# Transposed weights in a two-layer decode backward pass: turned by TensorE, or by the DMA on the way in

## The chip, the cores and the metric

The kernel runs on one core of a Trainium2 chip. The time is that of one execution on the device, in microseconds (us), and a kernel's time is the median of its runs. Engines are written as in the profile: PE is TensorE's matmul queue and PEld its weight loads, DVE is VectorE, ACT is ScalarE, POOL is GpSimd, SP is SyncE. SP issues all loads here and POOL issues all stores; both use the core's 16 DMA engines.

## The reference

Two layers of attention and MLP with the same weights and the same K/V caches, one query token for each of two batch rows, and then the gradient of everything. All tensors are bf16.

```python
x = A_x                                     # [2, 1, 1024]
x = x + A(ln(x), k_cache, v_cache, wq, wo)  # layer 0: attention
x = x + B(ln(x), w1, b1, w2, b2)            # layer 0: MLP
x = x + A(ln(x), k_cache, v_cache, wq, wo)  # layer 1
x = x + B(ln(x), w1, b1, w2, b2)            # layer 1
# A: q = x @ wq -> 32 heads of 128; k_cache, v_cache [2, 4, 16384, 128], 8 query heads per kv head
#    softmax(q k^T / sqrt(128)) v, then @ wo [4096, 1024]
# B: gelu(ln(x) @ w1 [1024, 3584] + b1) @ w2 [3584, 1024] + b2
# outputs: x, and the gradients of A_x, k_cache, v_cache, wq, wo, w1, b1, w2, b2 for a given grad_out
```

The products are thin (two columns), so the work is moving weights and caches through the chip: each K and V cache is read once in every pass of each layer, and the gradients of both caches, 33.5 MB each, are written at the end.

## The kernel before, in words

**Chunks and slots.** All that is read from HBM comes in chunks of up to 1 MB, 128 partitions by 4096 bf16. The program is first recorded as a list of pieces by `emit(fn, uses)`, each naming the chunks that it uses. `Program.run` then walks the list: it gives chunks, in the order of their first use, to slots as these come free, and issues a chunk's load the moment that it has a slot. So the order of the loads on SP is the order of first use, and a load is issued as early as slots allow. There are 14 slot tiles, three more areas in `last`, and four borrowed from `e1` and `ds1` while these are not in use. In the last pass six of the slot tiles are taken over as staging for the stores. The order on every engine is the order of the list; no scheduler changes it. A load waits on SP for the readers of its slot, and for the load eight places earlier.

**Turning on TensorE.** A product with a transposed weight needs the weight with its rows and columns exchanged. TensorE makes that: eight 128x128 transposes against an identity into a PSUM bank (`tp`), and one copy of 128x1024 to SBUF, on ACT or DVE, whichever has less counted work (`copy_bf`, L192 and L195). K and V blocks are turned in the same way. There are two forms:

- `ablock` (with `turn_of`, L324): the turn is emitted at once into a small tile `kT`, and the product that uses it is put in a list, `pend`, and emitted two blocks later (`SKEW = 2`), so that the copy lies behind other work.
- `turned` and `turned_ahead` (L365): the turned block is copied back over the chunk in its own slot (L368 on ACT, or L192 and L195), and the product reads it from the slot later.

**The two passes back.** Layer 1's backward attention is `attn_bwd(1, ...)`, and layer 0's `attn_bwd(0, ...)`. Each has 128 steps, 16 for each of eight (batch, kv head) groups, and 13 more for the second half of the work, which lags by 13 steps (`LAG_B`). A step turns a block of V and multiplies it (L940), multiplies a block of K (L921), and in some steps takes a block of wo (L807) or of wq (L836): 8 blocks of each weight for each of the four kv heads. The wo blocks of the first kv head come before the steps, the wq blocks of the last kv head behind them (`tail_wq`).

In layer 1 the steps from 86 on also turn w2 in its slots (L365, with the forward product L1229). Between the layers come, in this order: the LayerNorm's backward sums (L395), the products with the turned w2 (`w2_use`, L1257), between them the turns of w1 (`w1_turned`), the products with the turned w1 (`w1_bwd`, L727), the MLP's LayerNorm with the turns of the first wo chunks and of V's first blocks in its gaps (`chain`), and the wo products (L807).

In layer 0 the steps also make the outputs: weight gradients (L1072) and cache gradients (L1025), each a matmul of 128x512 into PSUM, a cast to a staging tile on ACT or DVE (`cast_out`, L200 and L203), and a store of 512 KB from POOL (L1032, L1088).

The loads are these two helpers' (L291 and L296):

```python
nc.sync.dma_start(ap.rearrange("p (t d) -> p t d", d=128), src[g, :, c * 32:(c + 1) * 32, :])
nc.sync.dma_start(ap[:, 0:rb * n].rearrange("p (j n) -> p j n", j=rb),
                  W[j0 * 128:(j0 + rb) * 128, c0:c0 + n].rearrange("(j p) n -> p j n", p=128))
```

Of the kernel before, what the change touches and what calls it, by code (L numbers as in the profile page):

```python
# [21 lines left out]
SKEW = 2  # L22
# [81 lines left out]
def kernel(  # L104
# [70 lines left out]
    obanks = [half[1, 0], half[1, 1], sb[1][:]]  # L175
    st = {"tp": 0, "ob": 0, "blk": 0, "stg": 0, "qm": [0, 0], "act": 0.0, "dve": 0.0}

# [112 lines left out]
    def ld_kv(src, g, c):  # L290
        return P.chunk(lambda ap: nc.sync.dma_start(  # L291
            ap.rearrange("p (t d) -> p t d", d=128), src[g, :, c * 32:(c + 1) * 32, :]))

    def ld_rows(W, j0, rb, c0, n):

        return P.chunk(lambda ap: nc.sync.dma_start(  # L296
            ap[:, 0:rb * n].rearrange("p (j n) -> p j n", j=rb),
            W[j0 * 128:(j0 + rb) * 128, c0:c0 + n].rearrange("(j p) n -> p j n", p=128)))
# [41 lines left out]
    def ablock(tiles, use, uses, mids=(), hold=None):  # L340


        if hold is None:
            hold = {}
            emit(turn_of(tiles, hold), uses)
        for fn, us in mids:
            emit(fn, us)
        pend.append(lambda: use(hold["kT"]))
        while len(pend) > SKEW:
            emit(pend.pop(0))  # L350

    def aflush():
        while pend:
            emit(pend.pop(0))

# [18 lines left out]
    def as_tiles(dst, part):  # L374
        return dst.ap[:, part * 1024:(part + 1) * 1024].rearrange("p (a b) -> p a b", b=128)

    def turned_ahead(blocks, act=True):

        now, then = [], []
        for n, (tiles, use, uses) in enumerate(blocks):  # L380
            now.append(turned(tiles, uses, uses[0], n % 4, act))
            then.append((lambda use=use, c=uses[0], n=n: use(as_tiles(c, n % 4)), uses))
        return now, then

    def turned_wo(wo):
        now, then = turned_ahead(wo[0])
        return now, then + [(wo[1], ())]

# [138 lines left out]
    def attn_fwd(l, order, x_in, chunk_k, chunk_v, first=None, tail={}):  # L527
# [103 lines left out]
        for s in range(n_steps + 2):  # L631
# [36 lines left out]
            else:  # L668
                if pend:
                    emit(pend.pop(0))  # L670
                for fn, us in mids:
# [122 lines left out]
    def wo_bwd_blocks(l, k):  # L794

        ws = ld_wo(k)
        hold = {}

        def blk(r):
            c = ws[r // 4]  # L800

            def use(kT):
                if r == 0:
                    hold["raw"] = small.tile([128, 8, 2], F32, name="do_raw", bufs=2)
                ps = ob()[:, 0:2]
                for o in range(DJ):
                    PE.matmul(ps, lhsT=kT[:, o, :], rhs=gA_all[:, o, 2 * l:2 * l + 2], start=(o == 0),  # L807
                              stop=(o == DJ - 1))
                V.tensor_copy(out=hold["raw"][:, r, :], in_=ps)
                dve(0.15)  # L810

            return (lambda: [col(c, r % 4, 1024, o) for o in range(DJ)]), use, [c]

# [13 lines left out]
    def wq_bwd_blocks(l, k, first, acc):  # L827
        ws = ld_wq(k)

        def blk(j):  # L830
            c = ws[j // 4]

            def use(kT):
                ps = ob()[:, 0:2]
# [8 lines left out]

            return (lambda: [col(c, j % 4, 1024, r) for r in range(R)]), use, [c]

        return [blk(j) for j in range(DJ)]

    def attn_bwd(l, order, gT, chunk_v, first, outputs=None, after=None, extra={}, fill=()):
# [37 lines left out]
        for i, k in enumerate(kvs):  # L886
# [6 lines left out]
            if i + 1 < HKV:  # L893
                for n, b in enumerate(bl):
                    wb[32 * i + 18 + LAG_B + 16 + 2 * n] = b
            else:
                now, tail_wq = turned_ahead(bl, act=False)
                for n, p in enumerate(now):
                    extra[129 + n] = list(extra.get(129 + n, ())) + [p]

# [3 lines left out]
        while s <= n_steps or (outputs is not None and outputs(s, True)):  # L904
# [39 lines left out]
            else:  # L944
                for fn, us in side[:n] + mids + side[n:2 * n]:
                    emit(fn, us)
                if pend:
                    emit(pend.pop(0))
            rest = side[2 * n:]
            if s in wb:  # L950
                ablock(*wb.pop(s), mids=rest)
            else:
                for fn, us in rest:
                    emit(fn, us)
# [241 lines left out]

    emit(turn_round)
    wo_now, wo_then = turned_wo(wo_bwd_blocks(1, up[0] % HKV))
    for p in wo_now[:4]:
        emit(*p)  # L1200
    dmps = w1_bwd(1, w1T)
# [9 lines left out]
    v_now, v_first = turns_ahead(chunk_v(up[0], 0))  # L1211
    chain(g3_, 1, wo_now[4:] + v_now)
    for p in wo_then:
        emit(*p)
# [22 lines left out]
    for j, s_ in enumerate(turn_steps):  # L1237
        i = j // 4
        extra.setdefault(s_, [])
        if j % 4 == 0:  # L1240
            extra[s_].append(w2_last(i))
        extra[s_].append(turned(lambda j=j, i=i: [col(ws2c[i], j % 4, 1024, o) for o in range(DJ)], [ws2c[i]],
                                ws2c[i], j % 4, act=False))
    ws1c = ld_w1()
    attn_bwd(1, up, saved["g3"], chunk_v, v_first, extra=extra, fill=w1_turned(ws1c, 0, ws1c[0]))
    col_to_row(xM1, out_0.rearrange("b s d -> (b s) d"))

# [13 lines left out]
    for i in range(FJ // 4):  # L1261
        emit(*w2_use(i))
        for p in w1_turned(ws1c, i, ws1c[i], act=False) if 1 <= i < 6 else ():
            emit(*p)
    emit(lambda: V.tensor_tensor(out=dh_all[:, :, 0:2], in0=slopes[0][:], in1=dhps0, op=ALU.mult))
    for j in (6, 7):
        for p in w1_turned(ws1c, j, ws1c[j], act=False):
            emit(*p)
    dmps0 = w1_bwd(0, ws1c)
# [5 lines left out]

    wo_now, wo_then = turned_wo(wo_bwd_blocks(0, down[0] % HKV))
    v_now0, v_first0 = turns_ahead(chunk_v(down[0], 0))
    chain(g1_, 1, wo_now + v_now0)
    for p in wo_then:
        emit(*p)  # L1280
# [79 lines left out]
```

## Time and profile before

| what | value |
|---|---|
| median of 3 runs | 1194.04 us (1185.31 to 1196.43) |
| profiled execution, its own time | 1194.48 us |
| its span | 1192.7 us |
| PE busy | 1032.3 us (87%) |
| weight loads (PEld) | 859.1 us (72%) |
| DVE, ACT, POOL busy | 605.4, 554.8, 125.1 us |
| read from HBM, written | 352.37 MB, 98.62 MB, 378 GB/s over the span |
| transposes L324 from slots | 4224, 369.2 us of PE |
| loads of wq, wo, 1 MB each, to landing | 10.7 and 15.2 us (median, into slots) |

The forward passes take the first 460 us. Layer 1's backward attention lies at 480 to 680, the change of layers at 680 to 737, layer 0's backward attention with all the outputs at 737 to 1170, and the last stores behind it. A matmul's time in the rows is from issue to its modelled end, and neighbours overlap, so the distance between starts tells more than the mean. The busy share of the DMA engines counts the time in which packets are under way, and stands a little above 1 when all are in use; the rate beside it says what was moved.

### The profile page before, as it was taken

Reading aid. Unit: us, or ns where it says so; the run is one execution under the profiler, and the core shown is the slowest. Engines: PE = TensorE matmul, PEld = TensorE weight load, DVE = VectorE, ACT = ScalarE, POOL = GpSimd, SP = SyncE. Lnnn points to the kernel's source line nnn. Section 1 sums busy time; section 2 is a strip of 40 time slices with the busy share of each in tenths; the row PEclk is TensorE's granted clock in tenths of the full one; section 3 lists DMA queues with packets and bytes.
Section 4 is the critical chain, followed back from the end, with each engine's and each line's share of the span. In section 5 each row is a group of like instructions: output and inputs, shape, how many; then the busy total and the mean of one; then the engine's idle time right before and its main releaser. Section 6 shows DMA issues by size and latency. Waiting matters only on the chain. (4 is left out here: it accounts for less than half of the span.)

```text
span 1192.7 us, 44045 instructions
## 1 busy us (share of the span) xinstructions
PE 1032.3 (87%) x19762; PEld 859.1 (72%) x19805; DVE 605.4 (51%) x1266; ACT 554.8 (47%) x996; POOL 125.1 (10%) x214
## 2 busy tenths in 40 slices
PE   6878887689988988888889988988997998899996
PEld 6778786688988987888888886655565555555663
DVE  2423242224333333333434435877886787677775
ACT  2423241124333423333444424766775776567774
POOL 1000000000000000000000010322222222222222
PEclk9966695679787758889999997999998999899998
DMA  9999999989999996999999976899999999999994
GB/s 365 420 421 421 422 420 421 386 298 378 420 420 420 422 409 264 378 414 418 417 402 330 365 295 232 323 376 373 417 417 373 384 417 410 371 362 409 416 415 200
DMA packets 106041, 453.83 MB, mean 381 GB/s; under 512 B 8658, under 2 KB 8658, under 8 KB 75516
## 3 DMA queue, kind: packets, MB, share of 16 engines
q1 hardware_dynamic: 78780, 352.36, 74.5%
q0 software_dynamic: 27072, 98.66, 20.5%
q8 instruction: 154, 2.52, 0.8%
q14 instruction: 35, 0.29, 0.1%
HBM read 352.37 MB, written 98.62 MB: 378 GB/s over the span
## 5 line engine op out<-in xcount | busy, mean ns | idle before, releaser
L192 ACT COPY kT<-tp 128x512 int32<-128x512 int32 x427 | 250.0, 586 | 418.3 <-PE tp L324 391.0
L324 PE MATMUL tp<-ident,slot 128*128 128x128 bf16 x4224 | 369.2, 238 | 12.1 <-issue 5.1
L324 PEld LDWEIGHTS <-slot 128*128 128x128 bf16 x4224 | 284.4, 107 | 30.0 <-issue 12.3
L195 DVE COPY kT<-tp 128x1024 bf16<-128x1024 bf16 x209 | 144.5, 691 | 296.6 <-PE tp L324 240.8
L200 ACT CAST slot<-sc 128x512 bf16<-128x512 f32 x271 | 157.6, 589 | 50.2 <-PE sc L1072 19.6
L203 DVE CAST slot<-sc 128x512 bf16<-128x512 f32 x227 | 154.4, 688 | 38.1 <-PE sc L1025 18.6
L1025 PE MATMUL sc<-last 128*128 128x512 bf16 x324 | 119.7, 389 | 17.1 <-ACT slot L200 5.3
L921 PEld LDWEIGHTS <-slot 128*128 128x128 bf16 x1888 | 80.0, 98 | 42.5 <-issue 18.6
L940 PEld LDWEIGHTS <-kT 128*128 128x128 bf16 x2048 | 80.7, 97 | 38.5 <-issue 21.4
L1032 POOL DMA_DIRECT2D out_dram<-slot x128 | 69.0, 539 | 281.2 <-ACT slot L200 173.9
L203 DVE CAST slot<-sb 128x512 bf16<-128x512 f32 x126 | 86.7, 688 | 18.1 <-PE sb L1025 6.4
L664 PE MATMUL sc<-qd,kT 128*128 128x8 bf16 x2048 | 90.3, 171 | 2.6 <-issue 2.6
L940 PE MATMUL sc<-qd,kT 128*128 128x8 bf16 x2048 | 90.0, 170 | 1.7 <-issue 1.6
L200 ACT CAST slot<-sb 128x512 bf16<-128x512 f32 x128 | 75.3, 589 | 29.1 <-PE sb L1072 16.0
L664 PEld LDWEIGHTS <-kT 128*128 128x128 bf16 x2048 | 73.1, 99 | 3.0 <-issue 2.9
L1025 PE MATMUL sb<-last 128*128 128x512 bf16 x161 | 62.1, 386 | 6.6 <-ACT slot L200 1.6
L365 PE MATMUL tp<-ident,slot 128*128 128x128 bf16 x692 | 58.0, 239 | 6.2 <-issue 2.2
L647 PE MATMUL sb<-e,slot 128*128 128x8 bf16 x1280 | 56.7, 176 | 6.3 <-ACT e L583 3.8
L1072 PE MATMUL sc<-last 128*128 128x512 bf16 x155 | 56.6, 384 | 4.8 <-DVE last L1060 3.3
L647 PEld LDWEIGHTS <-slot 128*128 128x128 bf16 x1280 | 50.1, 102 | 9.6 <-issue 7.1
L365 PEld LDWEIGHTS <-slot 128*128 128x128 bf16 x692 | 48.2, 107 | 11.5 <-issue 9.0
L192 ACT COPY slot<-tp 128x512 int32<-128x512 int32 (+1 forms) x52 | 29.7, 574 | 52.9 <-PE tp L365 49.8
(292 smaller groups left out, 1258.7 us busy)
## 6 DMA issues: line engine op xcount, KB each, us to landing
slot<-in_A_k_cache_dram SPq DMA_DIRECT2D x101, 1024.0 KB, 10.2
slot<-in_A_v_cache_dram SPq DMA_DIRECT2D x91, 1024.0 KB, 12.1
out_dram<-slot POOLq DMA_DIRECT2D x182, 512.0 KB, 10.3
slot<-in_A_wq_dram SPq DMA_DIRECT2D x28, 1024.0 KB, 10.7
slot<-in_A_wo_dram SPq DMA_DIRECT2D x23, 1024.0 KB, 15.2
last<-in_A_v_cache_dram SPq DMA_DIRECT2D x16, 1024.0 KB, 14.4
slot<-in_B_w_dram SPq DMA_DIRECT2D x18, 896.0 KB, 13.7
slot<-in_B_w_dram SPq DMA_DIRECT2D x12, 1024.0 KB, 12.5
```

The costliest lines, as they stand in the source:

```text
L192: S.copy(out=dst.bitcast(I32), in_=src.bitcast(I32))
L195: V.tensor_copy(out=dst, in_=src)
L200: S.copy(out=dst, in_=src)
L203: V.tensor_copy(out=dst, in_=src)
L324: PE.transpose(tp[:, j, :], t, ident[:])
L365: PE.transpose(tp[:, j, :], t, ident[:])
L647: PE.matmul(acc, lhsT=c.ap[:, ((vi % 4) * 8 + j) * 128:((vi % 4) * 8 + j + 1) * 128], rhs=e[:, vi, :, j], start=(vi == 0 and j == 0), stop ...
L664: PE.matmul(sc[t // 64][:, :, t % 64], lhsT=kT[:, j, :], rhs=qd[:, 0, g, l, :], start=True, stop=True)
L921: PE.matmul(sb[0][:, 0:8], lhsT=c.ap[:, ((vi % 4) * 8 + j) * 128:((vi % 4) * 8 + j + 1) * 128], rhs=d[:, vi, :, j], start=(vi == 0 and j = ...
L940: PE.matmul(scb[0][t // 64][:, :, t % 64], lhsT=kT[:, j, :], rhs=qd[:, 1, g, l, :], start=True, stop=True)
L1025: PE.matmul(ps, lhsT=hold["blk"][:, 2 * (hc % 2) + u // 2, :], rhs=flat(qms[w][:, (u % 2) * 4:(u % 2) * 4 + 4, :]), start=True, stop=True)
L1032: GP.dma_start((dKv if w == 0 else dVv)[g, :, hc * 16:(hc + 1) * 16, :], stg.rearrange("p (t d) -> p t d", d=128))
```

## The change

The weights that the backward passes need turned alone, wo and wq in both layers and w1 in layer 0, are loaded by `nc.sync.dma_start_transpose`: rows and columns are exchanged on the way from HBM into the slot. The products read the slot. The transposes on TensorE and the copies out of PSUM that made these tiles go away, 1248 and 160. A chunk of wo is 512 rows by 1024 columns, one of wq 512 rows by the 1024 columns of a kv head, one of w1 128 rows by 3584 columns. The block's product is emitted where the turn stood (`tblock`), no longer two blocks later; `pend` now counts blocks of both kinds, so the K/V products keep their distance in blocks. Layer 1's w1, used forward and backward, and w2 are turned on TensorE as before, and so are K and V.

```diff
+    def ld_turned(W, rows, cols):
+        n = (cols.stop - cols.start) // 128
+        m = rows.stop - rows.start
+        return P.chunk(lambda ap: nc.sync.dma_start_transpose(
+            ap[:, 0:n * m].rearrange("p (o m) -> p o m", o=n), W[rows, cols]))
...
-        pend.append(lambda: use(hold["kT"]))
-        while len(pend) > SKEW:
-            emit(pend.pop(0))
+        pend.append((st["turns"], lambda: use(hold["kT"])))
+        old_turns()
+
+    def old_turns():
+        st["turns"] += 1
+        while pend and pend[0][0] < st["turns"] - SKEW:
+            emit(pend.pop(0)[1])
+
+    def tblock(use, uses, mids=()):
+        for fn, us in mids:
+            emit(fn, us)
+        emit(use, uses)
+        old_turns()
...
     def wo_bwd_blocks(l, k):
-        ws = ld_wo(k)
+        ws = [ld_turned(A_wo, slice(k * 1024 + i * 512, k * 1024 + i * 512 + 512), slice(0, D)) for i in range(2)]
...
-            def use(kT):
+            def use():
+                kT = c.ap.rearrange("p (o m) -> p o m", o=8)[:, :, r % 4 * 128:(r % 4 + 1) * 128]
...
     def wq_bwd_blocks(l, k, first, acc):
-        ws = ld_wq(k)
+        ws = [ld_turned(A_wq, slice(i * 512, i * 512 + 512), slice(k * 1024, (k + 1) * 1024)) for i in range(2)]
...
-                now, tail_wq = turned_ahead(bl, act=False)
-                for n, p in enumerate(now):
-                    extra[129 + n] = list(extra.get(129 + n, ())) + [p]
+                tail_wq = bl
...
             if s in wb:
-                ablock(*wb.pop(s), mids=rest)
+                tblock(*wb.pop(s), mids=rest)
...
-    wo_now, wo_then = turned_wo(wo_bwd_blocks(1, up[0] % HKV))
-    for p in wo_now[:4]:
-        emit(*p)
+    wo_then, wo_end = wo_bwd_blocks(1, up[0] % HKV)
...
-    chain(g3_, 1, wo_now[4:] + v_now)
-    for p in wo_then:
+    chain(g3_, 1, v_now)
+    for p in wo_then + [(wo_end, ())]:
         emit(*p)
...
-    ws1c = ld_w1()
-    attn_bwd(1, up, saved["g3"], chunk_v, v_first, extra=extra, fill=w1_turned(ws1c, 0, ws1c[0]))
+    ws1c = [ld_turned(B_w1, slice(j * 128, (j + 1) * 128), slice(0, F)) for j in range(DJ)]
+    attn_bwd(1, up, saved["g3"], chunk_v, v_first, extra=extra)
...
     for i in range(FJ // 4):
         emit(*w2_use(i))
-        for p in w1_turned(ws1c, i, ws1c[i], act=False) if 1 <= i < 6 else ():
-            emit(*p)
...
-    for j in (6, 7):
-        for p in w1_turned(ws1c, j, ws1c[j], act=False):
-            emit(*p)
     dmps0 = w1_bwd(0, ws1c)
...
-    wo_now, wo_then = turned_wo(wo_bwd_blocks(0, down[0] % HKV))
+    wo_then, wo_end = wo_bwd_blocks(0, down[0] % HKV)
     v_now0, v_first0 = turns_ahead(chunk_v(down[0], 0))
-    chain(g1_, 1, wo_now + v_now0)
-    for p in wo_then:
+    chain(g1_, 1, v_now0)
+    for p in wo_then + [(wo_end, ())]:
         emit(*p)
```

## The prediction

> **What bounds the kernel now.** I read the rates by stage first, then who holds the load queue (SP), then the order of time on TensorE (PE) around the two turning points of the backward pass. This is the table by stage; its columns are the busy times of PE, weight loads, DVE, ACT and POOL, the granted clock, the DMA engines' busy share and the rate moved.
>
> ```profile
> 480.00:610.00 130.00, 112.06 (x2684) 110.24 (x2682) 50.18 (x118) 50.93 (x87) 0.00 (x0) 0.90 1.01 408
> 610.00:680.00 70.00, 65.76 (x1658) 63.37 (x1659) 28.75 (x59) 31.31 (x54) 0.00 (x0) 1.00 0.95 354
> 680.00:737.00 57.00, 49.85 (x961) 45.02 (x961) 21.80 (x71) 17.17 (x31) 4.54 (x3) 0.79 0.74 281
> 750.00:1170.00 420.00, 379.95 (x5248) 246.69 (x5275) 324.28 (x565) 290.67 (x535) 106.94 (x184) 0.97 0.99 388
> ```
>
> The best stretches of the forward pass move 420 to 422 GB/s (slices of the page), so I call 421 full. The first 130 us of layer 1's backward attention (stage B) run at 408, which is 97% of full: the transfers bound them, and PE's clock sags to 0.90. The last 70 us (C) run at 84% with PE at 94%: PE bounds. The change of layers (D) has both idle at times. Layer 0's backward attention (E) has PE at 90% and 388 GB/s, 92% of full: PE is first, the transfers are close behind. A 1 MB load at 421 GB/s takes **2.5 us** of all engines (1.049 MB / 421).
>
> Now SP's order of time at the end of layer 1 (start, us, line, what):
>
> ```profile
> 656.47 0.38 SPq L296 DMA_DIRECT2D slot<-in_A_wq_dram  x1
> 659.22 2.98 SPq L291 DMA_DIRECT2D slot<-in_A_k_cache_dram  x2
> 666.11 0.33 SPq L296 DMA_DIRECT2D last<-in_B_w_dram  x1
> 669.97 11.51 SPq L296 DMA_DIRECT2D slot<-in_B_w_dram  x7
> 682.06 0.38 SPq L296 DMA_DIRECT2D slot<-in_A_wo_dram  x1
> 692.96 0.38 SPq L296 DMA_DIRECT2D last<-in_A_wo_dram  x1
> ```
>
> A plain issue holds SP for 0.33 to 0.38 us. The eight w1 loads go out over 15 us as slots come free. And PE's order of time in D:
>
> ```profile
> 702.24 0.83 PE L365 MATMUL tp<-ident,slot 128*128 128x128 bf16 x12 [0.39 <-DVE slot L195]
> 702.91 0.95 PE L1257 MATMUL sc<-gM_all,slot 128*128 128x2 bf16 x32
> 703.72 1.05 PE L365 MATMUL tp<-ident,slot 128*128 128x128 bf16 x16
> ...
> 715.25 3.60 PE L365 MATMUL tp<-ident,slot 128*128 128x128 bf16 x32
> 718.64 3.20 PE L365 MATMUL tp<-ident,last 128*128 128x128 bf16 x32
> 721.79 1.33 PE L324 MATMUL tp<-ident,slot 128*128 128x128 bf16 x16
> 722.96 0.34 PE L395 MATMUL sb<-lb_s,onesf 128*128 128x4 f32 x2
> 725.50 0.54 PE L807 MATMUL sc<-gA_all,slot 128*128 128x2 bf16 x16 [2.21 <-DVE gA_all L783]
> ```
>
> Between the w2 products (L1257) stand the turns of w1, and the LayerNorm sum L395 stands behind 64 turns of wo.
>
> **The change part by part.**
>
> Removed: eight 128-row blocks per head group, weight (wo, wq) and layer, 4 x 2 x 2 x 8 = 128 blocks of 8 transposes, plus 8 x 28 for w1: 1248 transposes with their weight loads, and 128 + 32 = 160 copies out of PSUM (586 ns on ACT, 691 ns on DVE). Eight transposes take 0.44 us of PE at full clock (L324 from 655.83 to the next matmul at 656.27 in PE's timeline).
>
> Added: 32 of the 1 MB loads and the eight 896 KB loads of w1 become transposing loads. The bytes stay; the cost of moving them, c per 1 MB, is what no row shows. **Lower end**: the plain load, 2.5 us; the trace gives no reason for a gain below it, since the same bytes pass the same engines. **Upper end**: a transposing load is 32 squares of 128x128, and if each costs SP what one issue costs now, 32 x 0.33 = 10.6 us. The only load in 256-byte pieces today, sel8's 32 KB, takes 5.8 us to land, less than the 10.2 us of a K load, so it bounds nothing. The ends are far apart and neither row is clearly nearer; I take the geometric middle, 5.1, rounded to **c = 5 us**, twice plain, as an estimate.
>
> The Trainium skill, "DMA: Bandwidth & Descriptors", section "Latency and other measured facts", puts a DMA transpose at 261 GB/s where the middle dimension isn't contiguous. That is 4.0 us per 1 MB, an estimate from that page, and the sum below would then be -9 us, 1185. No run here shows it yet.
>
> Stage B: of the 16 chunks of wo and wq, eight are issued between 486 and 567 (SP's timeline: four wo, four wq). The stage is full, so each adds c - 2.5: 8 x 2.5 = **+20 us**. The PE and copy time that leaves here is worth nothing. Four wo chunks go out before 480, ahead of a hole (DMA at 138 GB/s in 450 to 460): 4 x 2.5 = 10 us are hidden there; were the hole gone, they would cost 10. The four turned wo blocks that leave the MLP's LayerNorm chain at 470 gain nothing, since loads already run full from 463 on.
>
> Stage C: four wq chunks add 10 us to 70 x 354/421 = 58.9 us of transfer work. At the 97% that stage B reaches, 68.9 becomes 71 us: **+1**. PE's saving of 16 blocks (8 in the steps, 8 in the tail) x 0.44 = 7 us can't be had, because the transfers are late next.
>
> Stage D: on PE, 1.8 us of w1 turns leave the LayerNorm chain at 682, the seven w2 products take 7 x 0.81 = 5.7 us in place of 22.3 (686.4 to 708.7), and L395 no longer waits 6.3 us for wo: 24.7 us. But w1 must have landed. From 666 eight loads take 8 x 0.875 x 5 = 35 us, to 701; then one V (2.5) and two wo chunks (10) and an allowance of 2 us for the landing: 715.5, against 725.5 now for the first use of wo (L807): **-10 us**. At c = 2.5, SP's wait until 692.96 and PE's own 24.7 us give about 701, so -24.
>
> Stage E: six wo and eight wq chunks add 14 x 2.5 = 35 us to 420 x 388/421 = 387 us; 422 us at 97% is 435 against 420: **+15**. PE's 56 blocks x 0.44 = 24.6 us, and as many copies, are covered by that. The writes share the engines, so a delayed read here also delays staging; I price that at nothing, for the 97% contains it.
>
> Placed without cost: the products (L807, L836, L727) now wait for the landing themselves, with the rest of PE's order behind them. In the steps they stand where the turn stood, so the deadline is the same. The K/V product's PSUM copy now has two blocks, of which one is no turn, as cover: 0.21 + 0.20 + 0.44 + 0.21 = 1.06 us (widths of L921, L836, L324, L921 in PE's timeline), above a copy's 0.59 to 0.69; in B, bound by transfers, a miss is free; in E, should every copy of the 48 steps with a turned block first stand behind a cast of 0.69, it is 48 x (2 x 0.69 - 1.06) = 15 us. The four last K loads of each layer now go before the wq tail. At the end, wq's last use is at 1169 and the last loads now go out by 1142.4: 27 us of cover for 10 us of transfers.
>
> **Sum**: 20 + 1 - 10 + 15 = +26 us on the profiled 1194.48 us (span 1192.7), so 1220.5; the median of the runs, 1194.04, is 0.4 lower, so **1220**.
>
> **The rivals**, by the same four terms:
>
> 1. Turned loads cost near plain, and PE's relief counts. At c = 2.5: B 0, C -7 (PE's saving), D -24, E 387/0.97 = 399, -21: -52, **1142**. At 3.3: 6 - 6 - 24 - 9 = -33, 1161. At 4: 12 - 3 - 19 + 1 = -9, 1185. For it: bytes and engines are the same, and the 2 KB pieces of wq and wo run in forward slices at the same 420 as K's 8 KB. Against: PE's relief reaches only C, D and E. It decides below c = 4.3. The skill's "Advanced Engine Details and Errata", section "X-Bar Transpose (TRN2)", calls transposing DMAs as fast as regular ones, which is this rival; no trace here bears on it.
>
> 2. SP issues square by square and holds up the plain loads behind it. At c = 7.5: 40 + 11 + 12 + 51 = +114, **1308**; at 10.6: 65 + 24 + 40 + 96 = +225, 1419. For it: SP is one queue in order, and the eight w1 loads and the wo loads stand in a row before V. Against: a plain 1 MB issue costs SP no more than a small one. The skill's "VectorE: DVE Perf Modes", section "The three transpose paths", lists 1309 ns for one 128x128 square by DMA; in series that is 41.9 us per 1 MB, far beyond even this.
>
> 3. The two cancel: c from 3.95 to 4.65, within 1%, about 1195.
>
> That the change doesn't turn what it says is out: the changed program holds 40 transposing loads and 2496 fewer PE instructions, 2 x 1248.
>
> **Numbers.** Forecast (c 4.65 to 6.5) 0.35, about 1208 to 1270; rival 1 below 3.95 us 0.33; rival 3 0.15; rival 2 above 6.5 0.17. Faster by over 1% (12 us; about what runs from 1185 to 1196 can tell from no change) 0.33, same 0.15, slower 0.52. The range 1148 to 1330 reaches from c about 2.7 to 8 and leaves out some 0.1 on each side: most of rival 2 at 10.6, and the very lowest of rival 1. The forecast's own range is 1208 to 1270, since both signs hold much.
>
> **What would show it.** The rate in B falls from 408 while the DMA share stays near 1.0 (c above plain), or stays (rival 1). The landing of the turned loads: near plain's 10 to 15 us, or far above. SP's width of one turned issue: 0.4 us, or several (rival 2), with the plain loads behind it late. In D, L807's first use comes near 715 plus B's and C's delay, released by DMA. In E, PE waits for DMA appear, where now there are almost none. The forecast is wrong if transposing loads drain between plain loads with gaps, so that c is set by the bubbles rather than the rate, or if the writes slow them further in E than in B.

## The result: 1395 us; between the faster runs 15.8% slower

| | before | after |
|---|---|---|
| median of the runs beside each other | 1193.76 us | 1395.19 us |
| ratio, with its 95% interval | | 1.158 (1.144 to 1.171) |
| profiled execution (span) | 1194.48 (1192.7) | 1403.27 (1401.2) |
| start of layer 0's backward attention (first product of its preparation, L981 before and L987 after) | 728.5 | 743.7 |
| from there to the end of the span | 464.2 | 657.5 |

The medians are of all runs; the ratio, here and in every table below, is between the faster runs of each kernel (here 1373.88 and 1387.12 us, a loss of 187; the other two took 1403.27 and 1409.87), and the profiled execution is one of the slower ones, with a loss of 208.

The forecast was 1220 us, with a range from 1148 to 1330: wrong in size, right in sign. The loss isn't spread out. In the profiled execution the changed kernel is 15.2 us late up to the start of layer 0's backward attention (stage E); in E it loses another 193.3.

These are the busy and DMA rows of the page of the changed kernel, 40 slices of 35 us. The slices from the 22nd on are stage E.

```profile
PE   6888966989888788778547858745777387782713
...
DMA  9999999899999999999999989999999999999995
GB/s 373 422 419 420 422 421 380 295 417 418 423 419 299 388 317 347 324 404 320 311 238 243 307 366 372 240 177 233 384 237 314 263 310 422 256 317 210 253 135 134
DMA packets 249005, 453.66 MB, mean 324 GB/s; under 512 B 169042, under 2 KB 169042, under 8 KB 218492
```

The bytes are those of before. The DMA engines look busy nearly throughout, but what they move in E is far below 388 GB/s and uneven, between 134 and 422 by slice. There are some 160,000 packets more of under 512 bytes: a turned load travels in packets of 256.

The same by stage (PE, weight loads, DVE, ACT, POOL, clock, DMA share, GB/s). Stage D now ends at 744, and E is shown over its old length and over its new one.

```profile
480.00:610.00 130.00, 104.62 (x2420) 102.24 (x2418) 38.05 (x103) 39.18 (x67) 0.00 (x0) 0.75 1.09 342
610.00:680.00 70.00, 57.53 (x1305) 55.10 (x1304) 21.60 (x46) 22.89 (x40) 0.00 (x0) 0.82 1.07 368
680.00:744.00 64.00, 27.15 (x750) 24.95 (x747) 10.41 (x50) 1.48 (x3) 4.54 (x3) 0.52 1.14 240
750.00:1170.00 420.00, 288.76 (x3462) 173.88 (x3471) 230.72 (x406) 205.85 (x377) 81.91 (x138) 0.82 1.10 293
750.00:1380.00 630.00, 404.09 (x4977) 245.26 (x4995) 322.01 (x568) 285.43 (x521) 111.31 (x190) 0.80 1.11 277
```

In E the PE, 90% busy before, is at 69%, and the rate is 293 GB/s with the DMA share *above* 1. So the engines are occupied by packets that do not move. Two pieces of the trace show how the program sees it. First SP's order of time, in layer 1 (one line), at the change of layers (two), and in a stretch of E:

```profile
535.68 20.24 SPq L298 DMA_TRANSPOSE slot<-in_A_wo_dram  x1
...
692.49 4.33 SPq L298 DMA_TRANSPOSE last<-in_B_w_dram  x1
696.91 30.36 SPq L298 DMA_TRANSPOSE slot<-in_B_w_dram  x7
```

```profile
881.37 22.58 SPq L298 DMA_TRANSPOSE slot<-in_A_wo_dram  x1
904.03 37.02 SPq L298 DMA_TRANSPOSE slot<-in_A_wq_dram  x1
941.15 0.53 SPq L291 DMA_DIRECT2D slot<-in_A_v_cache_dram  x1
...
942.79 3.37 SPq L291 DMA_DIRECT2D slot<-in_A_k_cache_dram  x1
946.26 34.38 SPq L298 DMA_TRANSPOSE slot<-in_A_wq_dram  x1
```

A turned load holds SP until over half of its own packets are under way (2448 of 4096 in the load issued at 483.12): 4.3 us each for w1 (30.36 / 7), where hardly anything else moves, and 22 to 37 us each in these lines of E. What stands ahead of it in SP's queue counts too: in layer 1, without a store in flight, one load holds SP for 20.24 us from 535.68, in which 7.1 MB of plain loads go by first. The plain loads behind it go out in a burst when it ends. Second, the longest waits of E in which a load or a store is waited for:

```profile
PEld L844 <- DMA slot<-in_A_wq_dram: 94.3, 6, 25.2
...
POOL out_dram L1038 <- DMA out_dram<-slot: 52.0, 13, 16.1
PE sb L844 <- DMA slot<-in_A_wq_dram: 47.7, 2, 24.0
PE sc L844 <- DMA slot<-in_A_wq_dram: 44.4, 3, 24.4
```

L844 is the wq product: the weight loads wait there six times, 94 us in all and up to 25 us each, for a turned load. The two PE rows, 92 us, are largely the same waits seen from the other queue. POOL, which issues the stores, waits as well, for stores to land. Loads and stores hold each other up.

### The profile page after: what moved, and what is told of

It is laid out like the page before. It is cut to its first block, busy times and chain, and to the rows that moved or that the text cites. A ratio compares the mean times of both kernels' runs of the same rounds, so it can differ in the third digit from the quotient of the medians.

```text
span 1401.2 us, 41292 instructions
## 1 busy us (share of the span) xinstructions
PE 1008.3 (72%) x18521; PEld 816.0 (58%) x18557; DVE 563.4 (40%) x1202; ACT 503.5 (36%) x900; POOL 125.5 (9%) x214
## 5 line engine op out<-in xcount | busy, mean ns | idle before, releaser
L192 ACT COPY kT<-tp 128x512 int32<-128x512 int32 x384 | 225.2, 586 | 561.7 <-PE tp L331 528.8
L331 PE MATMUL tp<-ident,slot 128*128 128x128 bf16 x3584 | 338.8, 251 | 35.4 <-DMA slot<-in_A_v_cache_dram 21.5
L331 PEld LDWEIGHTS <-slot 128*128 128x128 bf16 x3584 | 262.1, 113 | 54.5 <-DMA slot<-in_A_v_cache_dram 22.8
L195 DVE COPY kT<-tp 128x1024 bf16<-128x1024 bf16 x156 | 107.9, 691 | 281.3 <-PE tp L331 248.2
L1031 PE MATMUL sc<-last 128*128 128x512 bf16 x321 | 127.8, 425 | 17.7 <-ACT slot L200 10.1
L927 PEld LDWEIGHTS <-slot 128*128 128x128 bf16 x1888 | 84.0, 101 | 66.1 <-issue 39.9
L1031 PE MATMUL sb<-last 128*128 128x512 bf16 x172 | 72.5, 422 | 28.2 <-DVE last L1066 17.3
L844 PEld LDWEIGHTS <-slot 128*128 128x128 bf16 x448 | 16.5, 101 | 116.3 <-DMA slot<-in_A_wq_dram 106.0
L1078 PE MATMUL sc<-last 128*128 128x512 bf16 x159 | 63.8, 421 | 14.8 <-issue 6.2
L653 PEld LDWEIGHTS <-slot 128*128 128x128 bf16 x1280 | 50.5, 102 | 8.3 <-issue 5.7
L1031 PEld LDWEIGHTS <-last 128*128 128x128 bf16 x512 | 41.0, 103 | 22.2 <-issue 13.7
L927 PE MATMUL sb<-last,slot 128*128 128x8 bf16 x1024 | 47.6, 176 | 6.5 <-issue 6.2
```

Of the source, the lines that this page charges most:

```text
L192: S.copy(out=dst.bitcast(I32), in_=src.bitcast(I32))
L195: V.tensor_copy(out=dst, in_=src)
L331: PE.transpose(tp[:, j, :], t, ident[:])
L653: PE.matmul(acc, lhsT=c.ap[:, ((vi % 4) * 8 + j) * 128:((vi % 4) * 8 + j + 1) * 128], rhs=e[:, vi, :, j], start=(vi == 0 and j == 0), stop ...
L927: PE.matmul(sb[0][:, 0:8], lhsT=c.ap[:, ((vi % 4) * 8 + j) * 128:((vi % 4) * 8 + j + 1) * 128], rhs=d[:, vi, :, j], start=(vi == 0 and j = ...
L1031: PE.matmul(ps, lhsT=hold["blk"][:, 2 * (hc % 2) + u // 2, :], rhs=flat(qms[w][:, (u % 2) * 4:(u % 2) * 4 + 4, :]), start=True, stop=True)
```

## The experiments

Three theories were at hand for E. *Stores*: what slows a turned load is the stores in POOL's queue, taken in turn with it by the DMA engines. *Held queue*: SP, held by each turned load, issues the plain loads late, and that is the loss. *Row distance*: a turned load of wo or wq is dear by itself, because its rows lie far apart in HBM. The ratios below are against the kernel before, run beside each on the same chip.

### The loads by themselves

The first kernel leaves the computation out. Sections of eight loads and sixteen 512 KB stores follow one another. A section's stores wait for all that came before; its loads may begin while the last loads of the section before it land.

```diff
+        section(L(plain))
+        section(L(turned_wo))
+        section(L(turned_wq))
+        section(L(turned_w1))
+        section([], S(GP, 0))
+        section(L(plain), S(GP, 1))
+        section(L(turned_wo), S(GP, 2))
...
+        section([lambda i=i: (plain if i % 2 else turned_wo)(i) for i in range(8)])
```

> The computation is left out: this kernel only loads and stores, in 13 sections that wait for each other. The question is what eight transposing loads cost alone and beside other transfers. Three theories. Stores: a transposing load is slow only while POOL's stores are in flight. Then eight turned loads of wo, of wq and of w1 alone take 4.9 us per 1 MB (39 us for eight; w1 35), what the w1 loads show in the changed kernel between 692 and 727 us, and beside sixteen 512 KB stores they take well over 15 us each (above 120 us for eight), where plain loads beside the same stores take 8 x 2.5 + 16 x 1.25 = 40 us. Queue: the transposing load itself is as fast beside stores as alone, and the changed kernel loses because SP is held and loads behind it start late. Then the sections with stores take 39 + 20 = 59 us. Row distance: wq is slow because its rows lie 8 KB apart. Then wq alone takes twice the time of wo alone or more, with no store near. If it is POOL's way of storing, the section with the stores issued by ACT is as fast as the sum (59 us); if any second stream does it, also the one with plain loads issued by ACT is slow.

These are rates of its sections (DVE, POOL, clock, DMA share, GB/s): turned wo, wq and w1 alone, stores alone, plain loads with stores, and turned wo with stores, in two parts.

```profile
61.00:96.00 35.00, 2.34 (x53) 0.00 (x0) 1.00 1.13 238
96.00:132.00 36.00, 1.86 (x30) 0.00 (x0) 1.00 1.06 234
132.00:165.00 33.00, 2.04 (x40) 0.00 (x0) 1.00 1.05 215
165.50:189.20 23.70, 0.93 (x17) 8.61 (x16) 1.00 0.92 354
189.40:229.30 39.90, 2.44 (x40) 8.46 (x16) 1.00 0.99 381
235.00:261.00 26.00, 1.04 (x21) 8.46 (x16) 1.00 1.08 377
261.00:289.50 28.50, 1.09 (x8) 0.00 (x0) 1.00 1.10 239
```

A plain load follows the one before it after 2.7 us (DVE gets them at 50.00, 52.72, 55.43, 58.14 and 60.85). A turned one takes 4.4 to 4.5 us (1.049 MB at 238 and 234 GB/s), and wo, whose 512 rows lie one behind the other, costs the same as wq, whose pieces of 2 KB lie 8 KB apart. w1's 896 KB take 4.3 us. **Row distance falls.** The price of a turned load by itself, forecast at 5 us, is 4.4.

Beside stores the last two rows show a surprise without a crawl: in 26 us the stores went through at full rate and about one turned load (1.3 by its packets) with them; the other turned loads then ran at their own pace. The packets are 256 bytes on one side and 4 KB on the other, and about as many of each go by (517 and 459 in each 5 us from 240 to 255): the turned load starves until the stores are through, but the sum, 55 us, is about that of both alone. With the stores on ACT's queue the section takes 60 us, with stores whose rows in HBM are 512 bytes 66, and beside plain loads on ACT's queue 53. No 10 us of this kernel move less than 156 GB/s, where a sixth of E is below 140. So "stores" in this simple form was not enough: it expected above 120 us, and "held queue", which expected 59, came near.

### One layer at a time

```diff
+TURN = ['wo1', 'wq1']
...
-        ws = [ld_turned(A_wo, slice(k * 1024 + i * 512, k * 1024 + i * 512 + 512), slice(0, D)) for i in range(2)]
+        by_dma = f"wo{l}" in TURN
+        ws = [ld_turned(A_wo, slice(k * 1024 + i * 512, k * 1024 + i * 512 + 512), slice(0, D)) for i in range(2)] if by_dma else ld_wo(k)
...
-        ws = [ld_turned(A_wq, slice(i * 512, i * 512 + 512), slice(k * 1024, (k + 1) * 1024)) for i in range(2)]
+        by_dma = f"wq{l}" in TURN
+        ws = [ld_turned(A_wq, slice(i * 512, i * 512 + 512), slice(k * 1024, (k + 1) * 1024)) for i in range(2)] if by_dma else ld_wq(k)
```

This is the one with layer 1's wo and wq; the two others name layer 0's, and w1, in `TURN`. Where a load is plain again, the turn on TensorE and its place come back as before.

> wo and wq of layer 1 turned by the DMA; w1 and all of layer 0 on TensorE as before. Layer 1's backward pass has no stores. Stores: +15 to +22 us against the kernel before (8 x 2.4 in the full stage, nothing back), so 1209 to 1216. Queue: SP is held in layer 1 too, with the same number of transposing loads as layer 0, so about half of the whole loss, some +90 us. Row distance: wq's eight chunks lie here as well, so about half of the loss too.

> wo and wq of layer 0 turned by the DMA; w1 and all of layer 1 as before. Stores: nearly the whole loss, +170 to +195 us, 1365 to 1390. Queue and row distance: about half of it, +90 to +110.

> Only w1 of layer 0's MLP turned by the DMA. No stores run there but the first output row. Stores: eight loads of 4.3 us from 666 to 701 us, w1's products end near 703 in place of 715, the wo turns follow on TensorE as before: -8 to -12 us, 1182 to 1186. Queue: V's and wo's loads behind the eight start about 25 us later than before and the gain is eaten up: 0 to +10 us.

| turned by the DMA | median | ratio (95%) |
|---|---|---|
| wo, wq of layer 1, no stores in flight | 1214.36 us | 1.016 (1.012 to 1.019) |
| wo, wq of layer 0, all stores in flight | 1341.09 us | 1.111 (1.102 to 1.120) |
| w1 alone | 1193.31 us | 0.9985 (0.9955 to 1.0016) |

The same sixteen loads cost 19 us in layer 1 and 133 in layer 0 (0.0159 and 0.1111 of 1194.81, the median before beside them). SP is held in both. That speaks for the stores and against "held queue" and "row distance", which expected some 90 us in layer 1; layer 0 alone lost less than "stores" expected. With w1 the gain of 8 to 12 us that "stores" expected did not come; "held queue" had 0 to +10. These two rows of that kernel are the stretch from 680, where the loads of w1 are under way:

```profile
680.00:700.00 20.00, 16.79 (x514) 15.48 (x511) 5.44 (x24) 1.17 (x2) 0.57 (x1) 0.65 1.16 192
700.00:710.00 10.00, 1.81 (x56) 1.65 (x56) 0.00 (x0) 0.00 (x0) 0.00 (x0) 0.50 1.13 212
```

PE, relieved of the turns, waits for the loads; layer 0's attention starts at 729.9 instead of 728.5.

### Inside the crawl

The trace keeps every DMA packet with its queue, its bytes and the time it took. In the variant with layer 0's loads turned, one wq load (SP held from 864.62 to 888.25) shows three regimes one after the other. The rates come from the stage table of that kernel:

```profile
862.50:867.50 5.00, 0.00 (x0) 0.00 (x0) 0.00 (x0) 0.00 (x0) 0.00 (x0) 0.58 1.49 181
867.50:887.50 20.00, 15.55 (x182) 9.17 (x183) 12.68 (x22) 11.55 (x21) 4.25 (x8) 0.84 1.24 46
887.50:900.00 12.50, 1.53 (x11) 0.82 (x12) 1.59 (x3) 1.17 (x2) 1.61 (x3) 0.50 1.05 387
```

and the packets that start in 2.5 us from each moment are these:

```text
from us   turned packets (256 B)      store packets (4 KB)
          number   mean ns            number
857.5       253       27               214
862.5      1334       33                23
865.0      1505       45                11
867.5       113      216                13
870.0       274      180                15
872.5       245      199                14
880.0       274      194                14
885.0       275      194                15
887.5      1829       21                46
```

At 857.5 both queues have work everywhere: about one turned packet for one store packet, the store at full rate, the load starving, as in the sections above. At 865 the stores are nearly done and the load runs. From 867.5 to 887.5 *neither* runs: 46 GB/s for 20 us. The store packets are then 159 ns each and start 169 to 170 ns apart (880.111, 880.281, 880.450, 880.620, 880.789, 880.958), one at a time: 2500 / 170 = 14.7 in 2.5 us. That is one engine of the 16 at work on stores, with one turned packet between two of them by the counts. The turned packets of all the others, 16 x 14.7 = 235 in 2.5 us, took mostly 160 to 180 or 313 to 336 ns each: one or two of that engine's store packets.

The notices by which a store reports that it is done bear this out; there are 16 for each store, one for every eight of its packets. Of eight stores under way at 864.4 each had 15 notices. The last ones came one store at a time from 867.6 to 876.2, mostly some 1.4 us apart, which is eight packets of 170 ns: one engine is late with its share of all eight. From 877.6 to 888.1 the eight stores issued next got one notice each, and their other fifteen only from 891.3 on. So in the second half this engine was already at newer stores, while the other engines' shares of these stood still. Why they did isn't shown.

That gives a fourth theory. *Lockstep*: in a turned load all 16 engines advance together, and each waits, packet by packet, for the slowest. Then one engine with stores left brings the whole load, and with it SP and all loads behind, to that engine's pace.

### One engine with stores, on purpose

The second kernel without the computation has four turned loads (and, for comparison, four plain ones) beside 24 small stores on ACT's queue. A store of one row became one packet of 611 ns, that is, on one engine.

```diff
+    def rows(n, w):
+        def f(i):
+            nc.scalar.dma_start(flat2[0:n, i * 8192:i * 8192 + w], Z[0:n, 0:w])
+        return f
...
+        section(L(turned_wo, 4), L(rows(1, 8191), 24))
...
+        section(L(plain, 4), L(rows(1, 8191), 24))
```

> The computation is left out: sections of loads and stores follow one another. Four turned loads of wo, alone and beside 24 stores on ACT's queue that are uneven on purpose: one row of 16,382 bytes (which may fall to few of the 16 DMA engines), eight rows of 16 KB, one row of 16 KB. In the trace of the variant with layer 0's loads turned, turned packets of 256 bytes took 18 ns each where no store was beside them, and 173 to 336 ns in the stretch from 867 to 887 us, where store packets of 159 ns followed one another every 169 ns one at a time, as if a single engine still had stores. Lockstep (all engines wait in a turned load for the one that still has stores): while stores of a single engine run, the turned packets of all engines take a store packet's time, the rate falls under 100 GB/s, and a section with stores of few engines loses about the whole time of these stores beside 4 x 4.3 us. Plain sharing (only the engine that has stores is delayed): the turned packets of the other engines stay at 18 ns and most of the load's 4096 packets are through in 5 us, with the rest late. Plain loads beside the same stores should show no waiting on the other engines in either case.

The loads were not made to wait for the section's start, so those of one section ran beside the stores of the one before it; that changes which stores are beside them, not the comparison. The stores came too far apart to keep one engine busy, so the sections' lengths decide nothing. Single packets do. Packets that start in each 0.1 us, from 0.4 us before a store packet of 611 ns:

```text
beside turned loads, store packet at  65.00: 113 115 113 113 105 106  21   0   0   0   7  10  92 112 111 115
beside turned loads, store packet at  67.65: 113 112 117 113 106 104   5   0   0   0   7  12  96 111 103 114
beside plain loads,  store packet at 315.03:  18  24  19  17  18  23  18  16  18  22  19  13  16  22  19  16
beside plain loads,  store packet at 317.38:  22  19  18  21  20  18  17  18  19  16  19  21  20  18  18  19
```

One 16 KB packet on one engine stops the turned packets of all sixteen, from 113 in 0.1 us to none, until it is through; some 20 of them are recorded with 590 to 630 ns in place of 18. Plain loads, whose packets are of 2 KB here, do not notice it. Around the other store packets of this size beside turned loads the count fell to between 0 and 34, some of them at the seam of two loads. **Lockstep is shown** for single packets, and for a hardware queue: it needs neither SP's queue of plain loads nor POOL's software queue. What makes the engines wait for one another isn't shown.

### The stores in the loads' own queue

If two queues on one engine are what is dear, stores that stand in the same queue as the loads should be harmless. Three kernels issue the stores on SP: with all turned loads, with none, and with layer 0's alone.

```diff
-                            GP.dma_start((dKv if w == 0 else dVv)[g, :, hc * 16:(hc + 1) * 16, :],
+                            nc.sync.dma_start((dKv if w == 0 else dVv)[g, :, hc * 16:(hc + 1) * 16, :],
...
-                    GP.dma_start(out_ap[j0 * 128:(j0 + 2) * 128, c0:c0 + 1024].rearrange("(j p) n -> p j n", p=128),
+                    nc.sync.dma_start(out_ap[j0 * 128:(j0 + 2) * 128, c0:c0 + 1024].rearrange("(j p) n -> p j n", p=128),
...
-                    GP.dma_start(out_ap[j * 128:(j + 1) * 128, c0 + a:c0 + b], ap[:, 0:b - a])
+                    nc.sync.dma_start(out_ap[j * 128:(j + 1) * 128, c0 + a:c0 + b], ap[:, 0:b - a])
```

> The kernel before, with its stores issued by SP in the loads' queue: the base of sp_all. SP then waits for the data of a store with loads behind it, but 14 slots of loads stand ahead. Both theories: 1190 to 1250 us.

> The changed kernel, with the stores of the cache gradients and weight gradients issued by SP in the loads' own queue instead of by POOL in a queue of their own. Turns (the stores in the other queue, taken in turn with turned packets, are what makes layer 0's attention crawl): nothing is beside a turned load any more, it costs 4.3 us instead of 2.5, and this kernel stands 20 to 60 us above the same one without turned loads (sp_none), about 1200 to 1290 us by itself, well under the 1395 us of the change. Held queue (SP is held by a turned load, and what stands behind it is late): the stores now wait behind the turned loads as well, so it is 1395 us or more.

> Only layer 0's wo and wq turned by the DMA, stores in SP's queue. Lockstep: with nothing in another queue but instruction fetches, the 16 turned loads cost 4.3 to 5 us instead of 2.5, 29 to 40 us of transfers on a stage that is full to 97%, so 1215 to 1240 us. Against 1341 us of the same loads with the stores in POOL's queue. If the queue held by the turned loads were the cost, 1300 us or more.

| stores on | turned | median | ratio (95%) | from the start of layer 0's attention to the end |
|---|---|---|---|---|
| POOL | none (before) | 1193.76 us | 1 | 464.2 us |
| SP | none | 1192.85 us | 0.9986 (0.996 to 1.001) | 458.8 us |
| SP | layer 0's wo, wq | 1213.04 us | 1.013 (1.005 to 1.021) | 483.6 us |
| POOL | layer 0's wo, wq | 1341.09 us | 1.111 (1.102 to 1.120) | 608.1 us |
| SP | all | 1244.16 us | 1.042 (1.038 to 1.046) | 494.7 us |
| POOL | all (the change) | 1395.19 us | 1.158 (1.144 to 1.171) | 657.5 us |

Without turned loads the stores' queue makes no difference. With them it is worth, by the ratios, some 117 us (layer 0 alone) and 138 us (all). The last kernel of the three came out a little below the 1215 us at which its expectation began. Some turned loads of E in the kernel with all of them and the stores on SP:

```profile
844.09 6.44 SPq L299 DMA_TRANSPOSE slot<-in_A_wo_dram  x1
874.14 12.47 SPq L299 DMA_TRANSPOSE slot<-in_A_wo_dram  x1
891.10 7.07 SPq L299 DMA_TRANSPOSE slot<-in_A_wq_dram  x1
```

SP is still held, and now the stores stand behind the hold too; "held queue" expected 1395 us or more, and falls as the main cause. Of the turned packets in E, 22% took 100 ns or more with the stores on POOL, and 0.7% with them on SP. What is left with all turned loads, some 50 us, is 22 us up to the start of E and 30 in E against before, 13 and 36 against the same kernel without turned loads. With layer 0's alone E takes 19 us more than before, 25 more than the same kernel without turned loads. How much of this is the dearer loads and how much the holds was not separated.

### Without the stores

```diff
-                        if u == 3:
-                            GP.dma_start((dKv if w == 0 else dVv)[g, :, hc * 16:(hc + 1) * 16, :],
-                                         stg.rearrange("p (t d) -> p t d", d=128))
```

The stores of the weight gradients go in the same way.

> The changed kernel without its stores of the cache gradients and weight gradients (about 97 MB left out; the rest of the computation stays). Layer 0's attention backward then has some 72 MB of loads and is bounded by TensorE, which no longer turns 14 chunks there. Turns: 1000 to 1090 us, and the turned loads of that stage hold SP for about 5 us each where nothing is ahead of them. Held queue: holds of 20 us and more stay, and the time is 1150 us or more.

> The kernel before without its stores of the cache gradients and weight gradients (about 97 MB left out; the rest of the computation stays): the base of the changed kernel without these stores, which took 1189 us. Lockstep (the stores beside the turned loads make the loss): without stores the turned loads of layer 0 cost next to nothing, since that stage moves only some 200 GB/s there, and only the 15 us up to its start remain: this kernel takes 1165 to 1195 us. If turned loads cost layer 0's stage much even without stores: 1110 us or less.

With all turned loads 1189.22 us (ratio 0.994, 0.991 to 0.997), without any 1186.99 us (0.992, 0.989 to 0.995): no difference to speak of. The holds in E are these:

```profile
834.46 3.75 SPq L299 DMA_TRANSPOSE slot<-in_A_wo_dram  x1
862.11 5.26 SPq L299 DMA_TRANSPOSE slot<-in_A_wo_dram  x1
870.65 3.89 SPq L299 DMA_TRANSPOSE slot<-in_A_wq_dram  x1
895.60 3.77 SPq L299 DMA_TRANSPOSE slot<-in_A_wq_dram  x1
```

The expectation of 1000 to 1090 us for the first of the two was wrong, in a way worth noting: E hardly shrinks when its 97 MB of stores go. PE, 91% busy without them, bounds it with or without them (454.5 us without stores and turned loads, 464.2 before):

```profile
750.00:1170.00 420.00, 381.11 (x5287) 247.05 (x5315) 326.98 (x569) 293.87 (x541) 4.30 (x6) 0.98 0.49 169
```

That answers half of what the pair was for. The crawl needs the stores; but what turned loads cost by their own dearer transfers can't be read here, because E, without the stores and the turned loads, moves only 169 GB/s, the last number of this row. There PE's relief shows: with turned loads E takes 438.0 us, 16 less, which the 17 us of a later start take back.

### Half of w1

```diff
-    ws1c = [ld_turned(B_w1, slice(j * 128, (j + 1) * 128), slice(0, F)) for j in range(DJ)]
+    ws1c = [ld_turned(B_w1, slice(j * 128, (j + 1) * 128), slice(0, F)) if j % 2 == 0 else P_rows(j) for j in range(DJ)]
```

> Of all turned chunks only four of the eight of w1 come by the DMA (0, 2, 4, 6); TensorE turns the other four as before. With all eight by the DMA (1193 us, no difference) the stretch from 675 to 708 us waited for the DMA at some 200 GB/s, while before TensorE was busy 92% of it. Half of each should wait for neither: 1184 to 1192 us if that stretch bounds, 1193 us again if what follows it (layer 0's wo and the caches, which stand behind the turned loads in SP's queue) takes the gain back.

1192.41 us, ratio 0.997 (0.992 to 1.001): no measurable difference, between the two expectations. Layer 0's attention starts at 726.0 instead of 728.5, but this says little: in three kernels that do the same up to there it starts at 728.5, 733.4 and 737.1 (before, and without turned loads with no stores and with stores on SP). A gain of some 10 us isn't seen.

## Why the prediction was wrong

**The price of a turned load** was the open quantity, and it was nearly right: 5 us forecast by the middle of two bounds, 4.4 to 4.5 measured alone, and for w1 in the kernel 4.3 us for 896 KB, which is 5.0 per 1 MB. It was not what failed: by the prediction's own sum 4.4 us belongs to rival 3, about 1195 us, further from the result than 1220. The Trainium skill's "DMA: Bandwidth & Descriptors", section "Latency and other measured facts", gives 261 GB/s; the rows above show 238 and 234. The Trainium skill's "Advanced Engine Details and Errata", section "X-Bar Transpose (TRN2)", calls these DMAs as fast as regular ones, which was rival 1; it is contradicted by 4.4 against 2.7 us.

**Stage B (+20), C (+1).** Right in kind: the stage is full, and the rate falls from 408 to 342 GB/s. The first w2 product, at their end, comes 13.4 us later (699.8 against 686.4), not 21. The two other pairs that differ in the turned loads alone (stores on SP, no stores) show 10.6 and 13.9. Layer 1's loads alone cost the whole kernel 19 us.

**Stage D (-10).** The first use of wo was forecast 10 us earlier plus B's and C's delay, 725.5 - 10 + 21 = 736.5. PE's order of time has it at 738.0, released by the load as forecast:

```profile
737.96 0.59 PE L814 MATMUL sc<-gA_all,last 128*128 128x2 bf16 x16 [3.05 <-DMA last<-in_A_wo_dram]
```

By the measured delay of B and C the stage gained 1 us and not 10, so that 738.0 lies near the forecast by luck: two errors of 8 and 9 us cancel. In the two other pairs the stage is as long with turned loads as without, within 1 us. w1 alone brought no measurable gain either.

**Stage E (+15): the step that failed.** It priced the transfers (14 x 2.5 us at 97%) and then said: "The writes share the engines, so a delayed read here also delays staging; I price that at nothing, for the 97% contains it." What it put at nothing was worth some 163 to 174 us in the profiled execution (193 less the 19 to 30 below). The 97% could not contain it: it is the rate of stage B (408 of 421 GB/s), where only plain loads run and no store, and E itself ran at 92%. With stores in the loads' own queue the transfer term is fair: E then grows by 19 us with layer 0's loads turned and by 30 with all (forecast 15). With stores in a second queue, the packets of E after the change can be sorted, by each us between 743 and 1385, into these:

```text
stretch of E (1 us each)                                        us    GB/s   loss against 388 GB/s, us
40 or more store packets beside turned ones (load starves)     143    296    34
fewer stores, turned packets of 90 ns or more (lockstep)       144    108   104
between these                                                   65    153    39
turned packets alone, under 30 ns                               15    274     4
no turned packets, or 20 and fewer                             275    379     6
```

The loss of a row is its time x (1 - rate / 388). Together 187 us, against 193 that E grew; 143 of them lie in the second and third rows, where few stores and slow turned packets meet. That these are lockstep is argued from the packet times, by the pattern above; in the second row the mean is 19 store packets in a us, what some three engines move.

**The rivals.** The time fell where rival 2 put it, between 1308 and 1419, and SP *is* held by turned loads, with plain ones behind. But rival 2 needs a price of 7.5 to 10.6 us for each load, and it is 4.4, so its time was met by luck. The holds of E, up to 49.7 us beside stores, shrink to mostly 4 or 5 without them; the turned loads of layer 1, which hold SP for up to 20 us behind plain ones, cost 19 us in all. The sentence on what would make the forecast wrong named both real mechanisms, gaps and "if the writes slow them further in E than in B", and gave them neither a price nor a chance. No row of the trace of before prices them, since it holds no turned load; what it did show is that E is the one stage with stores in a second queue throughout.

**What stays open.** The records do not name the engine, so which one falls behind with its stores in E, and why, isn't shown. The stores on SP change three things at once (one queue instead of two, a queue that the profile calls hardware in place of software, and stores behind the holds); that two queues are enough was shown on ACT's hardware queue, for single packets. No run has this kernel's stores on ACT's queue, and eight loads beside sixteen stores there took 60 us, with no such crawl. The granted clock in E fell from 0.97 to 0.80, and the matmuls of the cache gradients took 425 ns in place of 389; PE is busy 69% of E, and what the clock adds to the loss was not separated. And why all turned loads with stores on SP cost 50 us when layer 0's cost 17 with the stores on SP and layer 1's 19 with them on POOL was not taken further.

## What to carry to other kernels

A DMA that transposes is not a plain load at a lower rate: by the runs here it takes 4.4 us instead of 2.7 for 1 MB, holds the queue that issues it until over half of it is under way, and waits on all DMA engines for one that is busy with another queue's packet, so such packets can cost far more than their bytes. Put it where nothing else is in flight, or keep the other transfers in its own queue (a ratio of 1.158 became 1.042 here). And count first what TensorE's turns really cost: none of the kernels with turned loads and all stores was measurably faster than before, and PE's relief showed only in E without stores, as 16 us. When a mean utilization is used as a price ("the 97% contains it"), ask whether the new kind of transfer belongs to the mix that gave it.

## What the hardware showed that was not expected

- A turned load stops on all 16 DMA engines while one of them has another queue's packet: 113 packets in 0.1 us fall to 0 within the 611 ns of one 16 KB store packet (to between 0 and 34 around the others); plain loads run on through the same.
- It holds its issuing queue: 4.4 us alone, 20 us behind 7.1 MB of plain loads, up to 49.7 us in one hold of E, where a plain issue mostly takes 0.33 to 0.5 us.
- Beside stores in another queue about as many packets of each go by, 256 bytes against 4 KB, so the turned load starves while the stores keep their rate (26 us of stores let through about one of eight loads).
- A busy share of the DMA engines above 1 together with a low rate was the sign: 1.24 at 46 GB/s in the crawl, where turned loads alone show 1.05 to 1.13 at 215 to 238. Packets that wait for one another count as busy.
- An instruction fetch slows it too: in a 16 KB fetch packet of 1.16 us at 703.14 in the changed kernel, the turned packets fell from 113 to between 8 and 59 in 0.1 us.
